# Twelve products of zeros ahead of TensorE's first work in a packed-attention and mixer kernel

## The chip, the cores and the metric

The kernel runs on one core of a Trainium2 chip. The metric is the time of one launch in microseconds, the median of several runs. The core has a matrix engine (TensorE, PE in the profile, with its weight loads as PEld), a vector engine (VectorE, DVE), an activation engine (ScalarE, ACT), a general engine (GpSimd, POOL) and a queue engine (SyncE, SP) that here issues all transfers between HBM and the on-chip memory. Each engine works through its own list of instructions in order.

## The reference

Eight batches, eight heads, 576 tokens, 64 numbers a head. A small set of 32 packing vectors per head first attends to all keys and values; then every query attends to the 32 packed vectors. The result, laid out as 576 x 512 per batch, goes through a low-rank mix over tokens and a two-layer channel network with residuals.

```
p_packed = softmax(scale * p @ k.T) @ v            # 32 x 64 per head
x        = softmax(scale * q @ p_packed.T) @ p_packed   # 576 x 512 per batch
u        = x + (x.T @ U @ V).T                     # U: 576 x 32, V: 32 x 576
out      = u + relu(u @ w_ch1) @ w_ch2             # 512 -> 2048 -> 512
```

U, V and the two weight matrices arrive as 64-bit floats and are turned into 32-bit floats on the chip from their bits.

## The kernel before, in words

The program has two parts.

The first part reads everything that the packed vectors need. There are 16 units (a batch and a group of four heads). For a unit, `a_load` (L396) brings the keys into a `kx` tile (three of them) and, at a batch's first unit, the packing vectors into `pn` (a single tile); `a_load_v` (L405) brings the values into `vt` (three tiles); `a_turn` (L427) transposes the keys on TensorE (L222, L232) and ACT and DVE copy them out (L229, L227, L233); `a_scores` (L435) multiplies them with the packing vectors (L242) into `s_ps`, of which there is one; `a_softmax` (L441) takes the maximum on DVE (L446, tile `mx`) and the exponential on ACT (L448); `a_turn_back`, `a_pack` and `a_heads` (L248, L476, L486) turn the exponentials, multiply them with the values and put the packed vectors where they are wanted. `a_p` (L415) prepares the packing vectors of a batch: a copy on POOL (L419, tile `pd`), two transposes (L421), and ACT (L422, L425). Between the units stand 16 pieces of the first weight matrix (`load_w1`, `test_w1`, `convert_w1`: L137, L143, and four DVE instructions L78 to L81 in `float32_of`), U and V (L197, L206), and from unit 6 on the steps of the first batch's query attention (`attention`, L253: `tokens` L310 and L311, `mix1` L318 to L322, `mix2` L330 to L333). At the end stand the first fold of weights (`fold`, L365: L370, L376, L377) and the first pieces of the second weight matrix (L151, L77, L158).

The order of this part isn't that of the text. A scheduler with a model of the machine lays it out: it puts every engine's instructions into the order in which its own reckoning has them start. An instruction more at one place can so move others on every engine.

The second part starts with `tc.manual_schedule()` (L559); from there on the order is that of the text. For each batch and each of 16 slices of the hidden layer it runs `gemm1` (TensorE products L86 to L88 into `h_ps`) and `gemm2` (L86 to L88 into `o`), each product as three products of split 32-bit numbers, with the remaining attention steps in between.

Two things of the first part matter below. `bank()` (L95) gives one of two PSUM banks named `t_ps`, and `conv_tile()` (L125) one of four SBUF tiles named `os`. The store of packed vectors of batch 1 and later to HBM (L492, tile `ppTa`, from ACT's L487) is issued by SP, in line with the loads.

Of the kernel before, what the change touches and what calls it, by code (L numbers as in the profile page):

```python
# [8 lines left out]
F32 = mybir.dt.float32  # L9
# [10 lines left out]
def packed_attention_mixer_kernel(  # L20
# [27 lines left out]
    nc = tc.nc  # L48
# [5 lines left out]
    P = 128  # L54
# [40 lines left out]
    def bank():  # L95
        return psT.tile([P, 512], F32, name="t_ps", tag="t")
# [28 lines left out]
    def conv_tile(dtype):  # L125
        return pipe.tile([P, DM], dtype, name="os", bufs=4)
# [83 lines left out]
    def load_nat(x, src, b, g):  # L210
        nc.sync.dma_start(
            out=x.rearrange("p (h y) -> p h y", h=2),
            in_=src[b, 4 * g:4 * g + 4].rearrange("(h z) (i c) d -> (z i) h (c d)", z=2, c=NT))
# [182 lines left out]
    def a_load(u):  # L396
        b, g = UN[u]
        ua[u] = {}
        if g == 0:
            pn[b] = sA.tile([P, 2, D], F32, name="pn", bufs=1)  # L400
            nc.sync.dma_start(out=pn[b], in_=p[b].rearrange("(g h) n d -> (h n) g d", g=2))
        ua[u]["x"] = sA.tile([P, 2 * S], F32, name="kx", bufs=3)
        load_nat(ua[u]["x"], k, b, g)
# [77 lines left out]
    def a_heads(u):  # L481
# [6 lines left out]
        if g == 1:  # L488
            if b == 0:
                ppT[0] = pps[0]  # L490
            else:
                nc.sync.dma_start(out=ppTd[b], in_=pps[b].rearrange("p g n -> p (g n)"))  # L492

    a_load(0)
    a_load(1)
    a_load_v(0)
# [265 lines left out]
```

## Time and profile before

| what | value |
|---|---|
| median of 3 runs | 845.87 us (845.39 to 845.93) |
| profiled execution, its time | 846.32 us |
| its span, first to last instruction | 844.5 us |
| PE busy | 814.8 us, 96% of the span |
| PE weight loads | 656.2 us, 78% |
| DVE, ACT, POOL busy | 377.1, 331.0, 86.9 us |
| DMA busy share in the first four of 40 slices (21.1 us each) | 90% or more |
| mean granted clock of TensorE | 0.993 of full |

The page gives busy time per engine, a strip of 40 slices, the transfers, the chain of waits that ended last, and groups of instructions. [...] The two parts of the program can be told apart in the strip: up to about slice 5 the transfers are busy all the time and PE is at six to nine tenths; from then on PE is full and the transfers are mostly idle.

### The profile page before, as it was taken

What the parts mean: (1) busy time and instruction counts of PE and PEld (TensorE: products, weight loads), DVE (VectorE), ACT (ScalarE), POOL (GpSimd) and SP (SyncE); (2) the same over time, 40 slices, a digit from 0 to 9 for tenths busy, and PEclk for the clock granted to TensorE, in tenths of its full rate; (3) what the DMA queues carried; (4) which work ended last, traced back from release to release, by engine and by line L of the source; (5) the groups of instructions that cost most, each with busy time, mean ns of one, the idle gap of its engine ahead of it and who ended that gap; (6) DMA issues with size and microseconds to landing.
All of it is one profiled execution on the core that took longest, in us unless ns stands there. A gap on an engine that the chain in (4) does not pass through costs nothing.

```text
span 844.5 us, 14606 instructions
## 1 busy us (share of the span) xinstructions
PE 814.8 (96%) x5800; PEld 656.2 (78%) x5800; DVE 377.1 (45%) x882; ACT 331.0 (39%) x1037; POOL 86.9 (10%) x131
## 2 busy tenths in 40 slices
PE   6887799999999999999999999999999999999997
PEld 4555478778878888888888888888788887888786
DVE  3888776984343333334343234333434234342221
ACT  4796664445233332334233332343234232332231
POOL 0122401100111000010011001010101011100000
PEclk9998999999999999999999999999999999999999
DMA  9999722331001100011001100110001100010001
GB/s 302 363 343 343 235 67 98 100 113 51 1 1 63 50 14 1 1 63 51 1 1 63 50 14 1 40 57 16 2 12 61 53 1 2 1 50 1 1 1 63
DMA packets 36245, 58.13 MB, mean 69 GB/s; under 512 B 9040, under 2 KB 19280, under 8 KB 36176
## 3 DMA queue, kind: packets, MB, share of 16 engines
q1 hardware_dynamic: 36176, 57.19, 20.5%
q8 instruction: 46, 0.75, 0.4%
q14 instruction: 23, 0.19, 0.1%
HBM read 46.83 MB, written 10.35 MB: 68 GB/s over the span
## 4 chain that ended last, share of the span: by engine, by line
PE 86%; DMA 5%; DVE 4%; issue 2%; ACT 2%; SPq 1%; POOL 0%; POOLq 0%; ACTq 0%; DVEq 0%
PE o L86 17%; PE o L88 16%; PE o L87 16%; PE h_ps L86 9%; PE h_ps L88 8%; PE h_ps L87 8%; PE t_ps L370 4%; DMA kx<-in_k_dram 2%; DMA bits<-in_moe_w_ch_dram 2%; PE t_ps L222 2%; DMA vt<-in_v_dram 1%; PE t_ps L242 1%; PE t_ps L318 1%; DVE os L80 1%; PE t_ps L248 1%
## 5 line engine op out<-in xcount | busy, mean ns | idle before, releaser
L86 PE MATMUL o<-w2h,hh 128*128 128x512 f32 x512 | 207.0, 404 | 0.0
L88 PE MATMUL o<-w2h,hl 128*128 128x512 f32 x512 | 202.7, 396 | 0.0
L87 PE MATMUL o<-w2l,hh 128*128 128x512 f32 x512 | 202.3, 395 | 0.0
L614 DVE SCALAR_TENSOR_TENSOR hl<-h_ps,hh 128x256 fp32r<-128x256 f32 x256 | 104.0, 422 | 202.1 <-ACT hj L613 189.8
L611 ACT ACTIVATE hh<-h_ps 128x256 fp32r<-128x256 f32 x256 | 98.7, 387 | 184.4 <-PE h_ps L88 183.9
L86 PE MATMUL h_ps<-ah,wth 128*128 128x320 f32 (+1 forms) x512 | 158.5, 310 | 1.7 <-DVE hl L614 1.7
L87 PE MATMUL h_ps<-al,wth 128*128 128x320 f32 (+1 forms) x512 | 152.4, 298 | 0.0
L88 PE MATMUL h_ps<-ah,wtl 128*128 128x320 f32 (+1 forms) x512 | 152.3, 297 | 0.0
L86 PEld LDWEIGHTS h_ps<-ah,wth 128*128 128x128 f32 x512 | 97.6, 191 | 34.5 <-issue 27.7
L88 PEld LDWEIGHTS o<-w2h,hl 128*128 128x128 f32 x512 | 96.6, 189 | 22.7
L86 PEld LDWEIGHTS o<-w2h,hh 128*128 128x128 f32 x512 | 97.0, 189 | 21.3 <-issue 4.6
L87 PEld LDWEIGHTS o<-w2l,hh 128*128 128x128 f32 x512 | 97.0, 189 | 16.7
L87 PEld LDWEIGHTS h_ps<-al,wth 128*128 128x128 f32 x512 | 97.6, 191 | 1.8
L88 PEld LDWEIGHTS h_ps<-ah,wtl 128*128 128x128 f32 x512 | 97.7, 191 | 0.0
L377 DVE TENSOR_TENSOR wtl<-t_ps,wth 128x256 fp32r<-128x256 f32 x128 | 48.5, 419 | 96.2 <-ACT wth L376 92.8
L376 ACT CAST wth<-t_ps 128x256 fp32r<-128x256 f32 x128 | 43.3, 374 | 109.5 <-PE t_ps L370 101.4
L333 POOL TENSOR_TENSOR al<-aT,ah 128x320 fp32r<-128x320 f32 (+1 forms) x32 | 26.3, 827 | 206.4 <-ACT ah L332 206.4
L281 POOL TENSOR_TENSOR e<-e,m 128x576 f32<-128x576 f32 x16 | 18.9, 1182 | 256.5 <-DVE m L280 256.5
L229 ACT COPY xT<-t_ps 128x256 f32<-128x256 f32 x64 | 21.4, 395 | 39.2 <-PE t_ps L222 38.5
L370 PE MATMUL t_ps<-w1t,ppT 64*32 64x512 f32 x512 | 36.0, 601 | 0.0
L332 ACT CAST ah<-aT 128x320 fp32r<-128x320 f32 (+1 forms) x32 | 13.6, 433 | 44.0 <-DVE aT L331 44.0
L292 POOL TENSOR_TENSOR e<-e,s 128x576 f32<-128x576 f32 x16 | 18.7, 1172 | 109.7 <-DVE s L291 109.0
(133 smaller groups left out, 956.8 us busy)
## 6 DMA issues: line engine op xcount, KB each, us to landing
bits<-in_moe_w_ch_dram SPq DMA_DIRECT2D x32, 512.0 KB, 6.4
kx<-in_k_dram SPq DMA_DIRECT2D x16, 576.0 KB, 7.0
x<-in_q_dram SPq DMA_DIRECT2D x16, 576.0 KB, 4.8
vt<-in_v_dram SPq DMA_DIRECT2D x32, 256.0 KB, 6.9
out_dram<-bits SPq DMA_DIRECT2D x32, 256.0 KB, 2.4
vt<-in_v_dram SPq DMA_DIRECT2D x16, 64.0 KB, 6.6
out_dram<-os SPq DMA_DIRECT2D x8, 128.0 KB, 2.4
ppTd<-ppTa SPq DMA_DIRECT2D x7, 128.0 KB, 2.5
```

Source lines behind the costliest of these rows:

```text
L86: nc.tensor.matmul(ps, lhsT=lh, rhs=rh, start=start, stop=False)
L87: nc.tensor.matmul(ps, lhsT=lh, rhs=rl, start=False, stop=False)
L88: nc.tensor.matmul(ps, lhsT=ll, rhs=rh, start=False, stop=stop)
L229: nc.scalar.copy(dst, src[:, a])
L281: nc.gpsimd.tensor_tensor(e, e, m.unsqueeze(2).to_broadcast([P, S // 32, 32]), op=ALU.subtract)
L292: nc.gpsimd.tensor_tensor(e, e, s.unsqueeze(2).to_broadcast([P, S // 32, 32]), op=ALU.mult)
L333: nc.gpsimd.tensor_tensor(al[:, g, ns], aT[:, ns], ah[:, g, ns].bitcast(F32), op=ALU.subtract)
L370: nc.tensor.matmul(f_ps[g][xs], lhsT=ppT[b][zs, g, xs], rhs=w1t[h // 2][zs, QW * c:QW * c + QW], start=True, stop=True)
L376: nc.scalar.copy(hi[:, g], f_ps[g][:, cs])
L377: nc.vector.tensor_tensor(lo[:, g], f_ps[g][:, cs], hi[:, g].bitcast(F32), op=ALU.subtract)
L611: nc.scalar.activation(hh[:, ms], src, AF.Relu)
L614: nc.vector.scalar_tensor_tensor(hl[:, ms], src, 0.0, hh[:, ms].bitcast(F32), op0=ALU.max, op1=ALU.subtract)
```

## The change

Just before the first loads are written, one `os` tile's first 128 columns are set to zero on DVE, one `t_ps` bank is taken, and twelve 128 x 128 x 128 products of these zeros with themselves are issued on TensorE. Nobody reads what they leave in the bank. Lines behind it move by six (L611 becomes L617).

```diff
+    zeros = conv_tile(F32)[:, :P]
+    nc.vector.memset(zeros, 0.0)
+    idle_ps = bank()
+    for _ in range(12):
+        nc.tensor.matmul(idle_ps[:, :P], lhsT=zeros, rhs=zeros, start=True, stop=True)
     a_load(0)
     a_load(1)
     a_load_v(0)
```

The scheduler lays the first part out anew; the order of the second part stays as it is on every engine. Three places are shown.

TensorE at the start of the program; the names are the tiles of the units 0 and 1. Before:

```order
L421 MATMUL t_ps<-ident,pd 128x128 x2
L222 MATMUL k_ps<-ident,kx 128x128 x8
L232 MATMUL k_ps<-ident,kx 64x128 x2
L242 MATMUL s_ps<-kT,pT 32x320
L242 MATMUL s_ps<-kT,pT 32x256
```

TensorE at the same place now:

```order
L499 MATMUL t_ps<-os 128x128 x12
L421 MATMUL t_ps<-ident,pd 128x128 x2
L222 MATMUL k_ps<-ident,kx 128x128 x8
L232 MATMUL k_ps<-ident,kx 64x128 x2
L222 MATMUL k_ps<-ident,kx 128x128 x4
L242 MATMUL s_ps<-kT,pT 32x320
```

The products of zeros stand in front, and half of the next unit's transposes has moved ahead of the first scores.

ACT some twenty microseconds before the end of the first part, from the first copies of `tokens` to the exponential of unit 13. Before:

```order
L310 CAST x<-t_ps 128x512 x2
L229 COPY kT<-k_ps 128x2x128 x3
L457 COPY eT<-m_ps 128x512
L460 COPY eT<-m_ps 64x128
L77 ACTIVATE os<-bits 128x512
L487 COPY ppTa<-t_ps 128x128
L233 COPY kT<-k_ps 64x4x64
L310 CAST x<-t_ps 64x256
L448 ACTIVATE e_1493,sm<-s_ps,mx 128x576
```

ACT there now:

```order
L310 CAST x<-t_ps 128x512 x2
L229 COPY kT<-k_ps 128x2x128 x2
L143 ACTIVATE os<-bits 128x512
L229 COPY kT<-k_ps 128x2x128
L457 COPY eT<-m_ps 128x512
L460 COPY eT<-m_ps 64x128
L233 COPY kT<-k_ps 64x4x64
L487 COPY ppTa<-t_ps 128x128
L310 CAST x<-t_ps 64x256
L478 ACTIVATE two<-m_ps,sm 128x128
L448 ACTIVATE e_1508,sm<-s_ps,mx 128x576
```

The test of a second-weight piece (L77) has gone from this stretch; a test of the last first-weight piece (L143) and the scaling L478 have come in.

DVE behind that, from the reciprocal of unit 13's sums to the maximum of unit 14 (L446). Before:

```order
L464 RECIPROCAL sm<-sm 128x2
L80 SCALAR_TENSOR_TENSOR os<-bits,os 128x512
L81 SCALAR_TENSOR_TENSOR os<-bits,os 128x512
L81 SCALAR_TENSOR_TENSOR w1t_83<-bits,os 128x512
L322 TENSOR_TENSOR ms<-t_ps,ms 32x256
L227 COPY kT<-k_ps 128x2x128
L331 TENSOR_TENSOR aT_1085<-t_ps,aT_1085 128x320
L446 TENSOR_REDUCE mx<-s_ps 128x1
```

DVE there now:

```order
L464 RECIPROCAL sm<-sm 128x2
L227 COPY kT<-k_ps 128x2x128
L322 TENSOR_TENSOR ms<-t_ps,ms 32x256
L78 TENSOR_SCALAR os<-os 128x512
L331 TENSOR_TENSOR aT_1100<-t_ps,aT_1100 128x320
L79 TENSOR_SCALAR os<-os 128x512 x2
L80 SCALAR_TENSOR_TENSOR os<-bits,os 128x512 x2
L446 TENSOR_REDUCE mx<-s_ps 128x1
```

The conversions have moved from ahead of L322 to behind it, and five of their instructions stand ahead of the maximum in place of three.

DVE at the end of the first part, up to the last split of the first fold (L377), behind which the second part begins. Before:

```order
L464 RECIPROCAL sm<-sm 128x1
L78 TENSOR_SCALAR os<-os 128x512
L79 TENSOR_SCALAR os<-os 128x512
L80 SCALAR_TENSOR_TENSOR os<-bits,os 128x512
L377 TENSOR_TENSOR wtl<-t_ps,wth 128x256
L81 SCALAR_TENSOR_TENSOR os<-bits,os 128x512
L446 TENSOR_REDUCE mx<-s_ps 128x1
L377 TENSOR_TENSOR wtl<-t_ps,wth 128x256 x3
```

DVE there now:

```order
L464 RECIPROCAL sm<-sm 128x1
L446 TENSOR_REDUCE mx<-s_ps 128x1
L331 TENSOR_TENSOR aT_1308<-t_ps,aT_1308 128x256
L78 TENSOR_SCALAR os<-os 128x512
L377 TENSOR_TENSOR wtl<-t_ps,wth 128x256
L79 TENSOR_SCALAR os<-os 128x512
L80 SCALAR_TENSOR_TENSOR os<-bits,os 128x512
L377 TENSOR_TENSOR wtl<-t_ps,wth 128x256
L81 SCALAR_TENSOR_TENSOR os<-bits,os 128x512
L377 TENSOR_TENSOR wtl<-t_ps,wth 128x256 x2
```

The maximum of unit 15 (L446) stands ahead of a whole conversion, which was half done before it. On ACT the exponential of unit 15, a cast and the piece's test now stand in a row ahead of the four casts of the fold:

```order
L457 COPY eT<-m_ps 128x512
L460 COPY eT<-m_ps 64x128
L448 ACTIVATE e_1717,sm<-s_ps,mx 128x576
L332 CAST ah<-aT_1308 128x256
L77 ACTIVATE os<-bits 128x512
L376 CAST wth<-t_ps 128x256 x4
```

Before, L77 stood eight rows ahead of that exponential, and the first three of the four casts ahead of it too.

## Rows read from the trace of the kernel before

**Rows 1.** Windows: stretch, length, busy (count) of each engine, PEclk, DMA share, GB/s.

```profile
4.00:86.00 82.00, 68.22 (x969) 45.42 (x969) 61.73 (x128) 59.06 (x189) 15.04 (x30) 0.96 1.06 349
86.00:92.00 6.00, 5.39 (x77) 4.03 (x79) 4.72 (x10) 4.44 (x14) 1.93 (x3) 1.00 0.37 86
104.20:110.00 5.80, 5.78 (x29) 5.35 (x30) 3.58 (x8) 3.28 (x10) 0.42 (x2) 0.71 0.20 78
200.00:844.50 644.50, 638.46 (x3967) 526.70 (x3965) 228.93 (x571) 209.70 (x674) 50.58 (x60) 1.00 0.07 25
```

**Rows 2.** Groups by form, PE, 0 to 22 us: count, busy us, mean ns, idle.

```profile
L222 PE MATMUL k_ps<-ident,kx 128*128 128x128 f32 x24 | 5.9, 426 | 1.2 <-DMA kx<-in_k_dram 1.2
```

**Rows 3.** The same, 24 to 62 us.

```profile
L222 PE MATMUL k_ps<-ident,kx 128*128 128x128 f32 x60 | 8.4, 279 | 0.7 <-ACT kT L233 0.5 <-DVE kT L227 0.2
...
L197 PE MATMUL t_ps<-os,x 128*128 128x144 f32 x8 | 1.2, 299 | 0.0
```

**Rows 4.** The same, 66 to 70 us.

```profile
L222 PE MATMUL k_ps<-ident,kx 128*128 128x128 f32 x8 | 1.9, 421 | 0.0
```

**Rows 5.** Timeline, 0 to 30 us: start, length, engine, line, idle before and releaser.

```profile
0.73 0.20 POOL masks.py:197 MEMSET ident<- 128x128 f32 x1 [0.29 <-POOLq L744]
...
3.27 0.69 PE L421 MATMUL t_ps<-ident,pd 128*128 128x128 f32 x2 [3.27 <-POOL pd L419]
...
5.14 1.97 PE L222 MATMUL k_ps<-ident,kx 128*128 128x128 f32 x8 [1.19 <-DMA kx<-in_k_dram]
...
14.09 0.37 SPq L211 DMA_DIRECT2D kx<-in_k_dram  x1
```

**Rows 6.** Transfers by line: count, KB each, median us from issue to landing.

```profile
kx<-in_k_dram SPq DMA_DIRECT2D x16, 576.0 KB, 7.0
```

**Rows 7.** Waits of the queue engine, 80 to 104 us: total, times, longest.

```profile
SPq L492 <- ACT kT L233: 3.9, 1, 3.9
```

**Rows 8.** Timeline, 72 to 113 us, ACT and DVE and PE.

```profile
84.09 1.06 ACT L310 CAST x<-t_ps 128x512 fp32r<-128x512 f32 x2
...
87.31 0.67 ACT L77 ACTIVATE os<-bits 128x512 f32<-128x512 f32 x1 [0.70 <-DMA bits<-in_moe_w_ch_dram]
...
88.55 0.74 ACT L448 ACTIVATE e<-s_ps,mx 128x576 f32<-128x576 f32 x1
...
90.48 0.17 DVE L464 RECIPROCAL sm<-sm 128x2 f32<-128x2 f32 x1
...
92.72 0.42 DVE L322 TENSOR_TENSOR ms<-t_ps,ms 32x256 fp32r<-32x256 f32 x1
...
94.20 0.72 PE L242 MATMUL s_ps<-kT,pT 64*32 64x320 f32 x4 [0.37 <-ACT pT L422]
```

**Rows 9.** Timeline, 95 to 108 us.

```profile
95.96 0.76 DVE L446 TENSOR_REDUCE mx<-s_ps 128x1 f32<-128x576 f32 x1 [1.81 <-PE s_ps L242]
...
104.23 0.39 PE L86 MATMUL h_ps<-ah,wth 128*128 128x320 f32 x1
```

**Rows 10.** Groups by form, DVE, 84 to 104.4 us.

```profile
L80 DVE SCALAR_TENSOR_TENSOR os<-bits,os 128x512 int32<-128x512 int32 x3 | 2.7, 887 | 0.0
...
L79 DVE TENSOR_SCALAR os<-os 128x512 int32<-128x512 int32 x3 | 1.8, 632 | 0.0
L81 DVE SCALAR_TENSOR_TENSOR os<-bits,os 128x512 int32<-128x512 int32 x2 | 1.6, 802 | 0.0
L377 DVE TENSOR_TENSOR wtl<-t_ps,wth 128x256 fp32r<-128x256 f32 x4 | 1.6, 412 | 0.6 <-ACT wth L376 0.6
...
L331 DVE TENSOR_TENSOR aT<-t_ps,aT 128x320 f32<-128x320 f32 x2 | 1.0, 486 | 0.1
L78 DVE TENSOR_SCALAR os<-os 128x512 f32<-128x512 f32 x2 | 0.9, 428 | 1.0 <-ACT os L77 1.0
```

**Rows 11.** Windows, 102 to 104 and 106 to 108 us, columns as rows 1.

```profile
102.00:104.00 2.00, 0.33 (x1) 0.14 (x1) 1.44 (x5) 1.17 (x5) 2.00 (x6) 1.00 0.37 84
...
106.00:108.00 2.00, 1.98 (x8) 1.69 (x8) 1.43 (x4) 1.47 (x3) 0.00 (x0) 0.50 0.00 0
```

## The prediction

> **What bounds the kernel now.** I read the strip first: transfers full for four slices, PE full afterwards. So I cut the span at the points where that changes [rows 1]. From 4 to 86 us the transfers' share is 1.06 at 349 GB/s, while PE is busy for 68.2 of 82 us, DVE for 61.7 and ACT for 59.1: this stage lasts as long as its loads. From 86 us the share falls to 0.37, and up to 104.23 us, when the first `h_ps` product starts [rows 9], a chain through DVE, ACT and PE sets the pace. From 200 us on PE is busy for 638.5 of 644.5 us. That part keeps its order, so the change can act on the time only by moving the point at 104.23 us, or TensorE's clock just behind it.
>
> Next I looked for the clock. The record has 1.00 in the first part, but a transpose of keys takes 426 ns in the first 22 us, 279 ns between 24 and 62 us, and 421 ns between 66 and 70 us, where the granted clock is 0.50 [rows 2 to 4]. [...] From row to row (busy time over count) a transpose costs 0.246 us at that level and 0.140 us at the higher one.
>
> **The zeros themselves.** The memset on DVE can start at 0.73 us and takes about the 0.20 us of POOL's memset of the same size [rows 5]; an estimate, as DVE shows none. Each product of 32-bit numbers is two passes: L197 is written four times and stands in the trace as eight [rows 3]. So there are 24 passes. At 0.246 us they last 5.9 us and end at 6.8; at 0.140 us they last 3.4 us and end at 4.3. Their real passes may be no longer than a transpose: L197 with 144 columns takes 299 ns beside 279.
>
> PE's first work was `pd` at 3.27 us, and the keys came at 5.14 [rows 5]. If the zeros end at 6.8, `pd` follows (0.69 us) and the keys start at 7.5 instead of 5.14, 2.4 us late; at best nothing is late. If the clock has risen by then, eight transposes take 1.1 us in place of 1.97, which gives back 0.9. I cost all this at nothing. What covers it is the backlog of loads: the next load that waits for a key tile to be freed is issued at 14.09 us, and from issue to landing a load of keys takes 7.0 us in the median [rows 6], of which its own 576 KB need only 1.7 at 349 GB/s, so some 5 us lie queued ahead of it. Without that cover the 2.4 us would be the price.
>
> The gain of an early clock is hidden by the same cover. The 24 transposes of keys in the first 22 us take 5.9 us [rows 2] and would take 3.4 at the higher level; I estimate as much again for PE's other work there, so 5 us. They lie beside loads. [...]
>
> **The new order of the first part.** By the order, SP issues 92 transfers ahead of the fourth store of packed vectors (L492), the same ones as before. The stage to 86 us moves the same bytes, so I leave its end where it is, and with it the state at 84.09 us, when `tokens` starts on ACT [rows 8]. That is an assumption; I give it 1 us either way.
>
> From there I replay the new order by hand with the old durations.
>
> First, to the maximum of unit 14 (L446). On ACT, L77 waited 0.70 us for its piece [rows 8]; now an L143 of the same form stands there whose piece was loaded sooner, so the wait goes, while L478 (about 0.4) comes in: 0.3 us sooner at L448. Between L464 and L446 stood 95.96 - 90.48 = 5.48 us [rows 8, 9], with an idle wait of 1.81 us for the scores. Now DVE has L464 0.17, L227 and L322 0.42 each, L78 0.43, L331 0.49, two L79 1.26 and two L80 1.77 [rows 8, 10]: 4.96 us, so 0.5 less if nothing is waited for. But L78 there needs L77, which on ACT now stands seven instructions behind L448. At half a microsecond each (two L310 take 1.06) it ends at 89.3 + 3.5 + 0.67 = 93.5, and then L78, L331, L79 and L80 (3.95) bring L446 to 97.4, or 1.4 later than 95.96. The ends are -0.8 (0.5 and 0.3) and +1.1 (1.4 less 0.3). Most of those seven ACT copies are smaller than L310, so I take a value nearer the lower end: -0.2.
>
> Second, from that maximum to the first `h_ps`. Before: 104.23 - 95.96 = 8.27 us. Now on DVE: L446 0.76, L81 0.80, two L331 0.98, L81 0.80, L464 0.17 and the maximum of unit 15, 0.76: 4.27. Then L331 runs beside ACT's L448 (0.74), L332 (0.41, as L377, which moves as much) and L77 (0.67): 6.09. L78 waits for that L77. Then L78 0.43, L377 0.41, L79 0.63, L80 0.89, L377 0.41, L81 0.80, two L377 0.82: 10.48. The same way of adding, with the old order and its 1.0 and 0.6 us of waits [rows 10], gives 9.16 for the measured 8.27, since neighbours overlap and one wait is covered; I take 0.9 off here as well: 9.6. That is 1.3 us more. Where the gain of the moved conversion goes: the maximum and exponential of unit 15 now stand in the chain, and the conversion behind them. The bounds: +0.8, if L79 and L80 are not stretched beside POOL (0.5 less), and +2.2, if the overlap isn't there.
>
> The sum: zeros 0, early clock 0, front -0.2, end +1.3: +1.1 us. Against the profiled execution, 846.32 us (span 844.5 and 1.8 around it), that is 847.4; that execution lies 0.45 over the median of the runs, so against the median 845.87 it is 847.0. The likeliest case's own range is +1.1 with the ends of both terms, -0.8 + 0.8 = 0 and 1.1 + 2.2 = 3.3: 845.9 to 849.2.
>
> **The rivals.**
>
> The chain gets shorter. For it: L322 stood 2.24 us behind L464 (92.72 and 90.48), because conversions were ahead of it; now only a copy is, so 1.8 us go, and PE's L330, the transposes of `pd` and the scores of unit 14 (94.20) come sooner by as much. ACT's 0.3 and the 0.5 us that SP then waits less of its 3.9 us at L492 [rows 7] add to it. If the conversions behind L322 sink into waits, and the end is no longer, this is worth -1.8 - 0.5 = -2.3 us: 843.6. Against it: DVE then still has the conversions before L446.
>
> The clock costs more, and the kernel is slower. Between 102 and 104 us PE was busy for 0.33 of 2 us, and at 106 to 108 the granted clock was 0.50 [rows 11]. Over 104.2 to 110 it was 0.71 on the mean [rows 1], so about 3.4 us at the lower level, in which PE loses 1.7 us of its products. If the end chain, with the maximum of unit 15 and a conversion in it, leaves PE idle for longer, the low stretch can double: +1.7 on top of +1.1, that is 848.7. It decides from the point at which PE falls idle behind the last scores for longer than before. Against it: the fold and the products with values are still there to be done in that gap.
>
> The early clock pays. If the zeros bring PE to the higher level before its first keys, and it stays there, the transposes run at 0.140 us each. [...] Were PE the bound of the first 22 us, the 5 us would go: 840.9. Against it stands the share of 1.06.
>
> That the zeros don't raise the clock at all (they may end too soon) is a rival in mechanism, but has the forecast's time, since the clock isn't on the path there.
>
> **How the numbers follow.** I give the forecast 0.45, the shorter chain 0.27, the clock behind 104 us 0.24, the early clock 0.04. A difference under 0.2%, 1.7 us, can't be told from none here. Of the forecast's range 0 to +3.3 about three quarters lie under +1.7: 0.34 same and 0.11 slower. The shorter chain gives 0.25 faster and 0.02 same. So faster 0.29, same 0.36, slower 0.35. For 8 in 10 the range goes from 843.0, just past the shorter chain, to 849.3, past the forecast's upper end and the clock case.
>
> **What would show it.** In the profile after: 24 passes of L499 from about 1 us; keys' transposes of 0.140 us pitch before 20 us, if the clock rose; a share of transfers near 1.06 to 86 us, whatever the clock does; L322 right behind L464; L446 of unit 14 near 96 us; the first `h_ps` near 105.3. The zeros' term is wrong if the transfers have a hole before 20 us. The order's term is wrong if `tokens` starts more than 1 us away from 84.09, since everything after hangs on it; and the whole is wrong if the stretch from the first `h_ps` to the end differs by more than the clock behind it explains.

## The result and the profile after

The changed kernel takes 849.32 us in the median of six runs (848.67 to 851.61), the kernel before in the same series 845.69 (845.39 to 846.34): a ratio of 1.0047, 95% interval 1.0034 to 1.0060. It is slower by 3.6 us. The forecast was 847.0, with a range from 843.0 to 849.3; the result lies just past its end. The profiled execution of after took 850.8 us (span 849.0), that of before 846.32 (844.5).

First the start. Timeline of after on TensorE and the queue engine, in the columns of [rows 5]:

```profile
1.05 5.49 PE L499 MATMUL t_ps<-os 128*128 128x128 f32 x24 [1.05 <-DVE os L496]
6.33 0.64 PE L421 MATMUL t_ps<-ident,pd 128*128 128x128 f32 x2
6.76 1.21 PE L222 MATMUL k_ps<-ident,kx 128*128 128x128 f32 x8
...
14.19 0.37 SPq L211 DMA_DIRECT2D kx<-in_k_dram  x1
```

The zeros are 24 passes. The eight transposes of keys behind them take 1.21 us instead of 1.97, that is 0.151 us each: near the 0.140 between 24 and 62 us [rows 3], where the granted clock is 1.00, and not the 0.24 at 66 to 70 us [rows 4], where it is 0.50. A granted clock of 1.00 is called the higher level here, 0.50 the lower. They start 1.6 us later than before, and the next load of keys is issued at 14.19 instead of 14.09. So the zeros did what they say, and nothing came of it.

Windows of after, columns as in [rows 1]:

```profile
4.00:86.00 82.00, 67.17 (x984) 44.45 (x984) 61.22 (x127) 59.75 (x188) 16.47 (x30) 0.94 1.07 348
14.00:20.00 6.00, 5.35 (x43) 3.45 (x31) 4.06 (x9) 4.12 (x14) 0.86 (x2) 0.50 1.07 347
...
94.00:96.00 2.00, 0.50 (x2) 0.19 (x1) 2.00 (x3) 0.54 (x2) 1.88 (x2) 0.96 1.05 389
96.00:98.00 2.00, 0.63 (x3) 0.63 (x4) 2.00 (x5) 1.51 (x4) 0.32 (x2) 0.50 0.59 182
98.00:100.00 2.00, 2.00 (x21) 0.61 (x19) 0.46 (x2) 1.23 (x4) 2.00 (x2) 0.50 0.85 271
...
104.00:106.00 2.00, 0.45 (x16) 0.20 (x14) 1.97 (x5) 0.65 (x2) 0.74 (x2) 1.00 0.00 0
106.00:108.00 2.00, 0.81 (x3) 0.55 (x4) 1.44 (x4) 0.81 (x3) 0.09 (x1) 0.52 0.03 12
108.00:110.00 2.00, 2.00 (x10) 2.00 (x10) 0.00 (x0) 0.52 (x2) 0.15 (x1) 0.50 0.82 274
110.00:112.00 2.00, 2.00 (x10) 1.94 (x10) 0.90 (x3) 1.22 (x5) 0.00 (x0) 0.50 0.16 50
```

The stage of the loads keeps its share, 1.07 at 348 GB/s. From 14 to 20 us the clock is at the lower level, 0.50, and the eight transposes at 16.30 us take 1.94 us: what the zeros raised is soon gone. Between 94 and 98 us PE is busy for 1.13 of 4 us and the clock is low until past 102 (0.50 from 96 on, 0.83 at 102 to 104); between 104 and 108 it is busy for 1.26 of 4 us and the clock is low again until past 112 (0.77 at 112 to 114). Before, PE was busy for 2.95 us in the first of these stretches, at a clock of 1.00; the second hole was there, shorter, at 102 to 104 us [rows 11].

DVE at the end of the first part in after, and the first product of the second part:

```profile
95.71 0.74 DVE L446 TENSOR_REDUCE mx<-s_ps 128x1 f32<-128x576 f32 x1
...
100.06 0.76 DVE L446 TENSOR_REDUCE mx<-s_ps 128x1 f32<-128x576 f32 x1 [1.60 <-PE s_ps L242]
...
102.65 1.26 DVE L78 TENSOR_SCALAR os<-os 128x512 f32<-128x512 f32 x1 [1.50 <-ACT os L77]
103.83 0.41 DVE L377 TENSOR_TENSOR wtl<-t_ps,wth 128x256 fp32r<-128x256 f32 x1
104.16 0.86 DVE L79 TENSOR_SCALAR os<-os 128x512 int32<-128x512 int32 x1
105.05 0.69 DVE L80 SCALAR_TENSOR_TENSOR os<-bits,os 128x512 int32<-128x512 int32 x1
...
107.45 0.42 DVE L377 TENSOR_TENSOR wtl<-t_ps,wth 128x256 fp32r<-128x256 f32 x1 [0.44 <-ACT wth L376]
...
107.76 0.61 PE L86 MATMUL h_ps<-ah,wth 128*128 128x320 f32 x1
...
113.42 0.39 PE L86 MATMUL o<-w2h,hh 128*128 128x512 f32 x1
```

The first `o` product of before:

```profile
109.23 0.39 PE L86 MATMUL o<-w2h,hh 128*128 128x512 f32 x1
```

Up to the maximum of unit 14 nothing is lost: 95.71 against 95.96 [rows 9]. From there to the first `h_ps` it takes 12.05 us instead of 8.27; I call this stretch the end below. From the first `h_ps` to the first `o` product it is 5.66 us (113.42 - 107.76) instead of 5.00 (109.23 - 104.23), at a granted clock of 0.50 to 0.52 from 106 to 112 us, where before has 0.71 on the mean over 104.2 to 110 [rows 1]. In sum 3.78 + 0.66 - 0.25 = 4.2 of the 4.5 us between the two spans.

Beside L78 stand POOL's memsets, and beside L79 POOL's split L333, in the same stretch of after:

```profile
100.95 1.00 POOL L581 MEMSET rdh<- 128x512 f32 x2
101.88 0.99 POOL L581 MEMSET rdl<- 128x512 f32 x2
102.81 0.56 POOL L581 MEMSET ajh<- 128x256 f32 x2
...
103.60 0.89 POOL L333 TENSOR_TENSOR al<-aT,ah 128x256 fp32r<-128x256 f32 x1
```

L78 starts at 102.65 and ends at 103.91. If its own work is the 0.43 us of [rows 10], that began at 103.48, just behind the `ajh` pair's end at 103.37. L79 starts at 104.16 and ends at 105.02; with the 0.41 us that it takes in e5 below, its own work began at 104.61, just behind the end of L333 at 104.49. L333 stands behind seven of the eight memsets in POOL's queue.

In before the conversion's L78 is ahead of the memsets:

```profile
98.25 0.43 DVE L78 TENSOR_SCALAR os<-os 128x512 f32<-128x512 f32 x1 [0.16 <-ACT os L77]
...
101.46 0.99 POOL L575 MEMSET rdh<- 128x512 f32 x2
```

### The profile page after: what moved, and what is told of

Its sections match the earlier page's. It is cut to its first block, busy times and chain, and to the rows that moved or that the text cites. A ratio compares the mean times of both kernels' runs of the same rounds, so it can differ in the third digit from the quotient of the medians.

```text
span 849.0 us, 14646 instructions
## 1 busy us (share of the span) xinstructions
PE 817.7 (96%) x5824; PEld 658.4 (78%) x5824; DVE 377.8 (45%) x883; ACT 332.2 (39%) x1037; POOL 88.0 (10%) x131
## 4 chain that ended last, share of the span: by engine, by line
PE 86%; DVE 5%; DMA 3%; ACT 2%; issue 2%; POOL 0%; SPq 0%; POOLq 0%; DVEq 0%; ACTq 0%
PE o L86 17%; PE o L88 16%; PE o L87 16%; PE h_ps L86 9%; PE h_ps L88 8%; PE h_ps L87 8%; PE t_ps L370 4%; PE t_ps L222 1%; PE t_ps L242 1%; DMA vt<-in_v_dram 1%; DVE os L80 1%; PE t_ps L318 1%; DMA bits<-in_moe_w_ch_dram 1%; DMA kx<-in_k_dram 1%; PE k_ps L222 1%
## 5 line engine op out<-in xcount | busy, mean ns | idle before, releaser
L617 ACT ACTIVATE hh<-h_ps 128x256 fp32r<-128x256 f32 x256 | 98.7, 387 | 184.8 <-PE h_ps L88 184.3
L377 DVE TENSOR_TENSOR wtl<-t_ps,wth 128x256 fp32r<-128x256 f32 x128 | 48.5, 419 | 96.0 <-ACT wth L376 92.7
L376 ACT CAST wth<-t_ps 128x256 fp32r<-128x256 f32 x128 | 43.3, 374 | 111.8 <-PE t_ps L370 101.4
L333 POOL TENSOR_TENSOR al<-aT,ah 128x320 fp32r<-128x320 f32 (+1 forms) x32 | 26.4, 829 | 209.0 <-ACT ah L332 209.0
L281 POOL TENSOR_TENSOR e<-e,m 128x576 f32<-128x576 f32 x16 | 19.2, 1201 | 255.9 <-DVE m L280 255.9
```

The costliest lines, as they stand in the source:

```text
L281: nc.gpsimd.tensor_tensor(e, e, m.unsqueeze(2).to_broadcast([P, S // 32, 32]), op=ALU.subtract)
L333: nc.gpsimd.tensor_tensor(al[:, g, ns], aT[:, ns], ah[:, g, ns].bitcast(F32), op=ALU.subtract)
L376: nc.scalar.copy(hi[:, g], f_ps[g][:, cs])
L377: nc.vector.tensor_tensor(lo[:, g], f_ps[g][:, cs], hi[:, g].bitcast(F32), op=ALU.subtract)
L617: nc.scalar.activation(hh[:, ms], src, AF.Relu)
```

## The experiments

Theory A says that the new order costs, not the zeros. Theory A's detail, which grew with the runs: the order puts a weight block's conversion (ACT's L77, DVE's L78 to L81) into the end of the first part, behind the maximum of unit 15 and beside POOL's memsets. The rivals: the zeros themselves cost, or the clock that they bring and lose. e1 to e15 were timed against the kernel before in five rounds each, on four chips, each beside runs of before on its own chip. "End" is the maximum of unit 14 to the first `h_ps` in the profiled execution. That is one execution of each; where an order has several, they show how far it can be trusted: 8.27 to 9.52 us in the old order (before, e1, e10, e12, e13), 12.05 to 12.07 in the new one (after, e2, e3).

| run | order of the first part | zeros | median us | ratio to before, interval | end us |
|---|---|---|---|---|---|
| before | old | 0 | 845.7 to 846.6 | 1 | 8.27 |
| after | new | 12 | 849.32 | 1.0047 (1.0034, 1.0060) | 12.05 |
| e1 | old | 12 | 846.99 | 1.0006 (0.9992, 1.0021) | 8.93 |
| e2 | new | 0 | 849.34 | 1.0035 (1.0021, 1.0049) | 12.05 |
| e3, gaps filled | new | 12 | 849.04 | 1.0029 (1.0015, 1.0043) | 12.07 |
| e4, conversion late | new | 12 | 847.08 | 1.0007 (0.9995, 1.0020) | 8.98 |
| e5, memsets late | new | 12 | 846.88 | 1.0016 (1.0007, 1.0024) | 10.79 |
| e6, one conversion per stage | old | 0 | 847.46 | 1.0021 (1.0009, 1.0033) | 6.63 |
| e7, as e6 | old | 12 | 847.93 | 1.0030 (1.0019, 1.0042) | 6.63 |
| e8 | a third | 24 | 850.52 | 1.0050 (1.0033, 1.0067) | 9.06 |
| e9, as e6, split late | old | 0 | 844.29 | 0.9981 (0.9971, 0.9992) | 6.64 |
| e10, memsets late | old | 0 | 846.25 | 1.0002 (0.9990, 1.0013) | 8.59 |
| e11, e9 and memsets late | old | 0 | 846.37 | 1.0004 (0.9992, 1.0015) | 6.63 |
| e12 | old | 4 | 846.74 | 1.0005 (0.9991, 1.0020) | 9.52 |
| e13 | old | 24 | 848.00 | 1.0027 (1.0012, 1.0042) | 9.15 |
| e14 | that of e8 | 0 | 850.80 | 1.0059 (1.0039, 1.0079) | 7.91 |
| e15, as e9 | new | 12 | 847.41 | 1.0016 (1.0004, 1.0027) | 8.96 |

### Zeros or order

e1 has the twelve products ahead of everything the planner sees, so that all other instructions keep the order of before. e2 takes them out behind the planner. e12 is the change with four products, for which the planner keeps the old order. In the diffs a line of dots stands for code left out.

```diff
 e1, ahead of the first part
+    with nc.psum_tensor([128, 512], F32) as idle_ps:
+        zeros = nc.const_aps.tensor(0.0, [128, 128], F32)
+        for _ in range(12):
+            nc.tensor.matmul(idle_ps[:, :128], lhsT=zeros, rhs=zeros, start=True, stop=True)
 e2, behind the planner
+    for b in nc.main_func.blocks:
+        b.instructions = [i for i in b.instructions if not (type(i).__name__ == "InstMatmult" and "t_ps_102_set" in str(i))]
 e12
-    for _ in range(12):
+    for _ in range(4):
```

> The twelve products of zeros run first on TensorE, but every other instruction stands in the order of the kernel before (the zeros come from a constant, so DVE's memset falls away). Theory A, the loss comes from the new order of the first part and the zeros cost nothing: 845.7 us, within 0.7 of the kernel before; tokens starts on ACT near 84.1 us and the first h_ps product near 104.2. Theory B, the loss comes from the zeros (first keys 1.6 us late, carried through, and more): 848 to 849.5. Theory C, an early clock pays once the order is left alone: 841 to 843.

> The changed kernel with the twelve products taken out after the order was laid out: every other instruction, DVE's memset too, stands where it stands in the changed kernel. Theory A (order): 849 us, as the changed kernel, with the first h_ps product at 107 to 108 us. Theory B (zeros): back to 845.7. Theory C would make it slower than the changed kernel, by up to 5 us.

> The change with four products of zeros instead of twelve, at the same place in the code. With four the planned order of all five engines is that of before but for the zeros and their memset. Theory A (the order that twelve bring about costs, the zeros do not): within 0.2% of before. Rival (a part of the cost is in the zeros themselves, in the buffer and the bank that they take from the rings, or in their memset at the start): 1 us or more over before.

Zeros with the old order (e1, e12): no difference from before. The new order without zeros (e2): as slow as after. DVE's row of e2 shows the same late and long L78:

```profile
101.15 2.12 DVE L78 TENSOR_SCALAR os<-os 128x512 f32<-128x512 f32 x1 [1.49 <-ACT os L77]
```

So the order costs, and at this count the zeros cost nothing that can be timed. An early clock bought nothing that can be timed either.

### Is it the clock in the end?

e3 puts products of zeros behind what PE waits for at three places between 94 and 106 us, ahead of the waiting instruction:

```diff
+    _fill(nc, {'I-1551': (8, 384, True), 'I-1741': (9, 0, False), 'I-1670': (2, 128, True)})
```

> The changed kernel with 8, 9 and 2 more products of the zero constant in TensorE's three gaps near 95 to 97, 104 to 106 and 106 us, which keep it busy there; the sums aren't changed by them. If the low clock after those gaps is what makes the end of the first part and the start of the second long (1.1 us on the scores of unit 15 and the transposes ahead of them, some 1.5 to 3 us in the first products of the second part): 846 to 847.5 us, the granted clock at 1.00 from 96 to 113 us. If DVE's chain of conversions sets it and the clock is beside it: 848.5 to 849.5, whatever the clock does.

A window of e3, columns as before, then ACT's and DVE's rows:

```profile
94.00:106.00 12.00, 9.02 (x113) 5.68 (x112) 9.10 (x16) 5.42 (x15) 7.80 (x15) 1.00 0.47 153
```

```profile
100.44 0.67 ACT L77 ACTIVATE os<-bits 128x512 f32<-128x512 f32 x1 [0.67 <-DMA bits<-in_moe_w_ch_dram]
...
101.14 1.64 DVE L78 TENSOR_SCALAR os<-os 128x512 f32<-128x512 f32 x1 [2.26 <-ACT os L77]
```

The clock stayed at 1.00 up to 106 us, and the maximum of unit 15 came 3.23 us behind that of unit 14 instead of 4.35. The end took 12.07 us all the same: L77 now waited for its transfer, and L78 for the memsets. POOL's rows say why no earlier maximum helps. The `ajh` pair in e2, then in e3:

```profile
102.18 0.56 POOL L581 MEMSET ajh<- 128x256 f32 x2
```

```profile
101.69 0.55 POOL L581 MEMSET ajh<- 128x256 f32 x2
```

It ends 7.66 us behind the maximum of unit 14 in after, 7.67 in e2 and 7.68 in e3. L78 starts 6.94, 6.08 and 6.58 us behind that maximum, and ends 8.20, 8.20 and 8.22 us behind it. So it ends when the memsets let it, whenever it was ready, and the three ends are alike (12.05, 12.05, 12.07). The clock ahead of the first `h_ps` is not what bounds this end; the conversion behind the memsets is. What the clock costs behind the first `h_ps` e3 doesn't tell: its record falls again there, to 0.55 at 106 to 108 us.

### The conversion and the memsets

e4 moves the conversion of block 1 behind the first `gemm1`. e5 leaves it and moves only POOL's memsets behind its copies L479; PE, DVE, ACT and SP keep after's order.

```diff
 e4
-    w2x = convert_w2(1)
+    w2x = None
...
             cur.gemm1(kt)
+            if (b, kt) == (0, 0):
+                w2x = convert_w2(1)
 e5
-    for t in (*rdh, *rdl, *ajh, *ajl):
-        nc.gpsimd.memset(t.bitcast(F32), 0.0)
...
+            if (b, kt) == (0, 1):
+                for t in (*rdh, *rdl, *ajh, *ajl):
+                    nc.gpsimd.memset(t.bitcast(F32), 0.0)
             if kt == 1:
                 cur.blocks()
```

> The changed kernel with the conversion of the second piece of the second weights written behind the first gemm1 instead of ahead of it; it leaves the end of the first part on DVE (L78 to L81) and ACT (L77), and the rest of the order stays. If DVE's chain sets the end: the four instructions took 3.5 us there (1.26, 0.86, 0.69, 0.68), so the first h_ps comes 2.5 to 3.5 us sooner and the time is 846 to 847 us. If the clock alone is the matter, PE still idles behind the scores: under 1 us less, 848.5 or more. If the conversion is only missed later (the second product of the second layer waits for it): no gain.

> The kernel after the change, with POOL's eight memsets of rdh, rdl, ajh and ajl moved from the end of the attention part (101 to 104 us) behind POOL's copies L479, so that none runs beside DVE's conversion L78 to L81; PE, DVE, ACT and SP keep the order of after. Theory A, first form (part of what makes the end of the attention part long is that POOL's memsets stretch DVE's L78: 0.43 us as its group's mean, 1.26 us in after, 2.12 us in the new order without zeros): L78 falls to about 0.45 us, the first h_ps comes 11.2 us behind L446 of unit 14 instead of 12.05, and the time falls by 0.8 us or somewhat more to about 848.5. Theory A, second form (the order alone: L78 waits for ACT's L77 and the rest of the chain follows whatever POOL does): L78 stays over 1.2 us or something else ends the chain at the same time, 12 us, 849.3 us.

DVE and PE in e5:

```profile
98.49 0.76 DVE L446 TENSOR_REDUCE mx<-s_ps 128x1 f32<-128x576 f32 x1 [1.60 <-PE s_ps L242]
...
101.07 0.49 DVE L78 TENSOR_SCALAR os<-os 128x512 f32<-128x512 f32 x1 [1.49 <-ACT os L77]
...
101.81 0.41 DVE L79 TENSOR_SCALAR os<-os 128x512 int32<-128x512 int32 x1
...
104.93 0.39 PE L86 MATMUL h_ps<-ah,wth 128*128 128x320 f32 x1
```

L78 falls from 1.26 to 0.49 us and L79 from 0.86 to 0.41 (POOL, with no memsets there, is busy for 0.74 us between 100 and 102 us and not at all between 102 and 104). `h_ps` starts at once at the higher clock (1.00 from 104 to 110 us; 0.39 us for what took 0.61 at 0.52), and `o` follows 3.87 us behind it instead of 5.66. The end gives 1.26 us of the gain, the clock behind it 1.79. About two thirds of the loss are gone by the ratios of e5 and after (half, by that of e2), without a change on any engine but POOL. L78 and L79 have one input each. By POOL's rows of after, L78 waited there for three memsets, up to 103.37 us: the second of `rdl` and both of `ajh`.

e4 takes the conversion out of the end altogether. The end is 8.98 us, 3.07 less than after, within the 2.5 to 3.5 expected, and the time is that of before within its interval. A part is given back: DVE then has two conversions in a row, and PE waits in the second stage.

```profile
113.50 0.41 PE L86 MATMUL h_ps<-ah,wth 128*128 128x320 f32 x1 [1.38 <-DVE hl L620]
```

e10 is e5's edit on the kernel before. There L78 and L79 (97.79 and 98.26 us) lie ahead of where the memsets were.

> The kernel before, with POOL's eight memsets moved behind its copies L479 as in the run of the new order with late memsets; the order of PE, DVE, ACT and SP is that of before. In before no L78 or L79 runs beside the memsets (101.46 to 104.4 us; L78 at 98.25 and L79 at 98.71 are ahead of them). Theory A (POOL's memsets cost only where DVE's L78 or L79 falls beside them, which the new order brings about): nothing gained, within 0.2% of before. Rival (the memsets cost in either order, by the copies L479 behind them or by any DVE work beside them): 1 us or more under before.

No difference, as theory A says. But the moved memsets meet a later conversion, in e5 and in e10. L78 of e5, then of e10:

```profile
113.01 2.13 DVE L78 TENSOR_SCALAR os<-os 128x512 f32<-128x512 f32 x1
```

```profile
112.99 1.38 DVE L78 TENSOR_SCALAR os<-os 128x512 f32<-128x512 f32 x1
```

PE is busy all the time in either run from 108 to 120 us: by the code (`convert_w2(kt + 2)` in the next diff) a block is converted two stages ahead of its use. So in these runs the memsets cost time only where a conversion falls beside them and TensorE's next work hangs on it soon.

### A better place for the conversion

e6 has one conversion in each stage of batch 0; e7 adds the zeros of e1. e9 is e6 with the split and the next load at the stage's end; e11 is e9 with e5's memsets.

```diff
 e6 and e9, on the kernel before
-    w2x = convert_w2(1)
+    w2x = None
...
             cur.gemm1(kt)
+            if b == 0 and kt + 1 < NK:
+                w2x = convert_w2(kt + 1)
...
-                if kt + 2 < NK:
-                    w2x = convert_w2(kt + 2)
 e9 alone: the split and load_w2(kt + 3) from there to behind add_u()
             if kt == 3:
                 cur.add_u()
+            if w2x:
+                split_w2(*w2x)
...
```

> The kernel before, with one conversion of a w2 block in each stage kt of batch 0, behind gemm1(kt), instead of the first ahead of the loop: L77 to L81 of block 1 leave the end of the attention part, and no stage has two conversions (in the run with the late conversion the second one held up hl L620 by 1.4 us at 113 us). Theory A (DVE's conversion in the end of the attention part holds up w1's pieces L377 and with them the first h_ps): L78 to L81 were 3.5 us of DVE time there, between L464 and L446 of unit 15, of which about 2 us are on the path; h_ps comes about 6.5 us behind L446 of unit 14 instead of 8.27, the low clock behind it is as long or shorter, and the time is 843 to 844.5 us (1 to 2.5 us under before). Rival (the end is set by PE's and ACT's chain from the scores to the transposes, as 8.98 us in the run with the late conversion suggest): h_ps stays 8 to 9 us behind L446 of unit 14, and the time is that of before, 845.7.

> The same as the run before it, and the twelve products of zeros ahead of everything with the order of before kept. Theory A (the zeros themselves are worth nothing that can be timed, the order of the end is): the time is that of the run without the zeros to 0.2%, whatever that is; the clock is high from the first transposes on. Rival (an early clock pays as soon as the end of the attention part does not eat it): 1 us or more under the run without zeros.

The end of e6 came out at the 6.5 us expected (6.63; without the conversion the planner also puts two of the fold's splits L377 ahead of the maximum of unit 15, in place of one), and the time did not: 847.46 where 843 to 844.5 was expected. ACT and PE of e6 show where it went:

```profile
111.41 0.62 ACT L158 CAST w2h<-os 128x512 fp32r<-128x512 f32 x1 [2.03 <-DVE os L81]
```

```profile
115.71 0.30 PE L250 MATMUL t_ps<-ident,e 128*64 128x128 f32 x1 [2.05 <-ACT xT L229]
```

L158 waits in ACT's queue for DVE's chain, and the copies that PE needs stand behind it. e7 agrees with e6 within its interval: the zeros are worth nothing here either.

> The kernel before with one conversion of a w2 block in each stage of batch 0 behind gemm1(kt) (as in the run with conversion per stage), and the block's split (L158, L159) and the next load at the end of the stage, behind blocks() and add_u(). In the earlier run the first h_ps came 2.3 us sooner than before (101.89 against 104.23) and the gain was lost at 113 to 116 us, where ACT's L158 waited 2.03 us for DVE's L81 and the copies of rdh, the relu and L229 stood behind it, so that PE's L250 waited 2.05 us. Theory A (the end of the attention part is set by DVE's conversion, and what is gained there stays if no engine's queue gives it back): no wait of 2 us at 113 to 116 us, 843.5 to 845 us, 1 us or more under before. Rival (DVE's and ACT's work in the first stages of the second part is the bound, so a conversion that leaves the end of the attention part must be paid for there): another wait of about the same length stands in PE's row within the next stages, and the time is 846 us or more.

> Both edits of the two runs before it together: conversion in each stage with the split at the stage's end, and the memsets behind L479. Theory A: with no conversion in the end of the attention part the memsets have nothing to hold up, so the time is that of the run with the split late to 0.2%. Rival: they add up, 1 us under it.

In e9 the same two rows read:

```profile
113.71 0.62 ACT L158 CAST w2h<-os 128x512 fp32r<-128x512 f32 x1 [0.23 <-DVE os L81]
```

```profile
116.18 0.30 PE L250 MATMUL t_ps<-ident,e 128*64 128x128 f32 x1 [0.22 <-ACT xT L229]
```

e9 is the one version that beats both kernels: 0.9981 (0.9971 to 0.9992) of before. e11 was to be the same and is not. Its memsets, moved, met the next conversion. DVE and POOL of e11:

```profile
110.72 2.45 DVE L79 TENSOR_SCALAR os<-os 128x512 int32<-128x512 int32 x1
113.20 0.69 DVE L80 SCALAR_TENSOR_TENSOR os<-bits,os 128x512 int32<-128x512 int32 x1
```

```profile
110.72 1.00 POOL L710 MEMSET rdh<- 128x512 f32 x2
111.65 0.99 POOL L710 MEMSET rdl<- 128x512 f32 x2
112.58 0.84 POOL L710 MEMSET ajh<- 128x256 f32 x2
```

L79 starts with the memsets and takes 2.45 us; L158 then waits 1.43 us and PE's L250 2.23 us, as in e6. An expectation that failed, for the cause that e5 had shown: here a block is converted one stage ahead of its use (`convert_w2(kt + 1)`), not two.

### Twenty-four zeros, and what is left

e8 is the change with `range(24)`; e14 takes these out behind the planner as e2 does; e13 is e1 with 24. e15 is e9's edit on the kernel after.

> Twenty-four products of zeros instead of twelve, at the same place in the code. The order that comes out is a third one: in the end of the attention part DVE's conversion L78 to L81 stands ahead of L446 of unit 15 and only the four L377 stand behind it. Theory A (the order decides, not the zeros): no conversion behind L446 of unit 15, h_ps at most 9.5 us behind L446 of unit 14, and the time is 845 to 847.5 us, under that with twelve. Rival (the zeros cost, by work or by what their clock brings): twice the zeros cost twice as much, 852 to 853 us, or at least not less than with twelve, 849.3 us or more.

> Twenty-four products of zeros in front, all other instructions in the order of before (as the run with twelve zeros in the old order). The kernel with twenty-four zeros and the order that they bring took 850.5 us although its end of the first part was no longer than 9.1 us: there the tokens' step L310 started at 87.1 us instead of 84. First reading (the order of the first 86 us made that late): the zeros end near 8.7 us, the keys' transposes start 3.5 us late and nothing else is late, tokens at 82 to 86 us, and the time is within 0.2% of before. Second reading (twenty-four zeros, which end at 8.6 us, hold up the loads behind the keys): 849 us or more, tokens at 86 us or later.

> The order that twenty-four zeros bring about, with the twenty-four products taken out behind the planning. First reading (that order costs): 849 us or more, tokens at 86 us or later. Second reading (the zeros cost): the time falls by 2 us or more against 850.5, tokens at 84 us.

I expected e8 near before, since its conversion stands ahead of the maximum of unit 15. Its end is short indeed (9.06 us), but `tokens` starts at 87.1 us instead of 84.1: this third order is late in the stage of the loads. e14 shows that this is the order's doing: without any zeros `tokens` starts at 86.93 us, and the kernel is as slow. The first `tokens` row of e8, then of e14:

```profile
87.14 0.60 ACT L310 CAST x<-t_ps 128x512 fp32r<-128x512 f32 x1
```

```profile
86.93 0.60 ACT L310 CAST x<-t_ps 128x512 fp32r<-128x512 f32 x1
```

e13 adds that 24 zeros, which end at 9.05 us, cost something by themselves, 1.0027 (1.0012 to 1.0042), where twelve and four cost nothing that can be timed. Neither of its two readings came out. Where the cost stands its profiled execution doesn't show (`tokens` at 83.49, end 9.15); it stays open.

> The kernel after the change, twelve zeros and its order of the first part, with one conversion of a w2 block in each stage of batch 0 behind gemm1(kt) and its split and the next load at the stage's end, as in the run with the split late (844.3 us on the order of before). L78 to L81 and L77 leave the end of the first part, and the memsets have nothing to hold up there. Theory A (of the new order only the conversion in the end of the first part costs, with the clock that falls in the gap behind it): h_ps about 9 us behind L446 of unit 14, as in the run with the late conversion, no wait of over 1 us at 112 to 116 us, and 845 to 846.5 us, at least 3 us under after. Rival (the new order costs elsewhere too, or what is taken out is given back in the stages that follow, as with the late conversion): 847 us or more.

e15 expected 845 to 846.5 us and took 847.41. Its end is 8.96 us where e9, the same edit on the old order, has 6.64. DVE of e15:

```profile
95.07 0.74 DVE L446 TENSOR_REDUCE mx<-s_ps 128x1 f32<-128x576 f32 x1
...
99.41 0.76 DVE L446 TENSOR_REDUCE mx<-s_ps 128x1 f32<-128x576 f32 x1 [1.60 <-PE s_ps L242]
...
101.70 0.42 DVE L377 TENSOR_TENSOR wtl<-t_ps,wth 128x256 fp32r<-128x256 f32 x1 [1.20 <-ACT wth L376]
```

DVE of e9:

```profile
97.55 0.76 DVE L446 TENSOR_REDUCE mx<-s_ps 128x1 f32<-128x576 f32 x1 [1.81 <-PE s_ps L242]
...
100.63 0.42 DVE L377 TENSOR_TENSOR wtl<-t_ps,wth 128x256 fp32r<-128x256 f32 x1 [0.95 <-ACT wth L376]
...
102.22 0.75 DVE L446 TENSOR_REDUCE mx<-s_ps 128x1 f32<-128x576 f32 x1
```

The two maxima are no further apart in e15 (4.34 us) than in e9 (4.67). What is longer is the stretch behind the second one: 4.62 us to the first `h_ps` instead of 1.97. In e9 two of the fold's four splits L377 stand ahead of that maximum; in e15 all four stand behind it, and their casts L376 behind unit 15's exponential in ACT's queue.

So the new order costs at two places: the conversion beside the memsets, and the fold behind the maximum and exponential of unit 15. Neither removal alone makes it a gain. The second place is read from e15 and e9; no run moves the fold alone, so it isn't shown by an experiment. The wait for the last scores at the lower clock isn't a third one that the runs show: in e2, with the same order and a granted clock of 0.94 at 96 to 98 us, where after has 0.50, the maxima are 3.50 us apart instead of 4.35, and the end is as long.

## Why the prediction was wrong

- **Zeros 0: right.** 24 passes were foreseen and are there. They end at 6.5 us (foreseen 6.8 at the latest), the next load of keys is 0.1 us later, and e1 and e12 show no difference.
- **Early clock 0: right.** The transposes took 0.151 us each (1.21 over 8) behind the zeros, against 0.246 in before (1.97 over 8 [rows 5]; the record has 1.00 there in both kernels, so the level is read from the transposes alone), and the share of transfers stayed at 1.07; e1 is not faster than before. Ahead of the low clock of before at 66 to 70 us (0.64 at 64 to 66, then 0.50) PE had waited for ACT (1.26 us, up to 63.93) and for POOL (0.53, up to 65.47).
- **`tokens` stays where it is: right for this change,** 83.90 against 84.09, and wrong as a rule: executions of old and new order had it between 82.3 and 86.5 us, and that of e8 and e14 at 87.
- **Front -0.2: right in the number, and in part by luck.** 95.71 against 95.96, but 0.19 of the 0.25 were there at `tokens`. Behind it two larger moves cancel: L464 came 0.93 us sooner, not the 0.3 that the sum has, and from there to the maximum it took 6.35 us instead of 5.48, with waits of 1.05 us for a copy of ACT's and 0.84 for L77. The rival of the shorter chain was right up to the scores of unit 14, which started 1.26 us sooner (92.94 against 94.20); DVE's conversions ahead of the maximum used that up, as the argument against it says.
- **End +1.3: the step that failed.** The term was the right one, and mis-sized: 9.6 us, with a bound of +2.2 on what it adds, and it measured 12.05, +3.8. By pieces: (1) maximum to maximum I added up DVE's own work, 3.51 us, and had the scores of unit 15 there in time; it was 4.35, with DVE waiting 1.60 us for them at the lower clock (0.50 from 96 to 100 us). (2) From the second maximum to L78 I had 2.58 and it was 2.59. (3) From L78 to `h_ps` I had 4.39, took 0.9 off for overlap, and it was 5.11: L78 took 1.26 instead of 0.43, L79 0.86 instead of 0.63, the last L377 waited 0.44 for ACT's L376, which wasn't in the sum, and neighbours overlapped by only 0.5. In sum 0.84 + 0.01 + (5.11 - 3.49) = 2.47, which is 12.05 less the unrounded 9.58. Piece (1) did not decide the end: in e2 it was 3.50, in e3 3.23, and the end the same, since the memsets held L78 whenever it was ready. I had POOL's hold on DVE in the sum for L79 and L80 only, as the group means of before had it (beside POOL's L333 at 98.64 us they took 1.08 and 1.10 us there), and did not look at what POOL would be doing beside the moved L78. POOL's order was there to be read.
- **The rival of the clock: its condition came true, its size did not.** PE fell idle for longer, as it names, and by the windows the low stretch doubled, from about 3.4 to 6.8 us, of which some 1.7 lie ahead of the first `h_ps`. Between the first `h_ps` and the first `o` that costs 0.66 us more than before, not 1.7: against the 3.87 us of e5, where the clock stays high, it is 1.79 in after and 1.13 in before. Its time, 848.7, is the nearest of those given, for the wrong sum: most of the difference to before is the chain that let PE fall idle (3.78 us in the end), and e3, with the clock high up to 106 us, has the same end.

## What to carry to other kernels

Where a scheduler sets the order, an edit is two edits: what is added, and the new order. Do the first without the second (place it outside the planner) before you judge either. Read a moved vector instruction not with its old duration but beside what the other engines will run there: L78 took 0.43 us in before [rows 10], and 1.26, 2.12 and 1.64 beside POOL's memsets in after, e2 and e3. And a piece of work that is taken out of a critical stretch is a gain only if the queue that it moves to has no wait in front of what TensorE needs next: e6 and e11 had an end 1.6 us shorter than that of before and were no faster, e9 was.

## What the runs showed of the hardware

DVE's L78 and L79 (one input) waited through several of POOL's back-to-back memsets. With 0.43 us taken for their own work, L79 of e11 came in 0.1 us behind the fourth memset (110.72 to 112.64), and took 2.45 us; L78 of after, e2 and e3 came in 0.1 us behind the sixth, and took 1.26, 2.12 and 1.64. Why behind the fourth here and the sixth there, no run shows. DVE's L80 (two inputs) took 0.69 beside the last memsets of e11, which is its median in before; but beside POOL's L281 (73.48 us in before) it took 1.53. The memsets beside the vector instruction that got in took longer themselves (the `ajh` pair of e11 0.84 us instead of 0.56). And behind 5.5 us of zeros TensorE's transposes took 0.151 us each, but between 14 and 20 us the granted clock was 0.50, after a wait of 1.90 us for ACT's exponential at 13 us.
